# Turning the first attention weights on TensorE, and an earlier start of the dense layer, in a fused attention and SoLU kernel

## Chip, cores, metric

The kernel runs on one core of a Trainium2 chip. The metric is the device time of one execution in microseconds (us), the median of several runs.

The engines are called by the names of the profile: PE (TensorE, matmul; PEld is its weight load), DVE (VectorE), ACT (ScalarE), POOL (GpSimd), SP (SyncE, which issues most DMAs).

## Reference

```python
# q, k, v: (8, 8, 576, 64) float32; tau a scalar
scores = scale * np.matmul(q, k.transpose(0, 1, 3, 2))
thresh = np.max(scores, axis=-1, keepdims=True) - tau
scores = np.where(scores >= thresh, scores, -1000000000.0)
attn = softmax(scores); x = attn @ v        # heads side by side: (4608, 512)
h = x @ w_in                                # w_in (512, 1024)
solu = h * softmax(h)
ln = (solu - mu) / np.sqrt(var + 1e-06) * g_ln
out = ln @ w_out                            # w_out (1024, 512)
```

`w_in` and `w_out` arrive as 64-bit floats. The kernel reads them as 64-bit integers and makes 32-bit floats of them itself.

## The kernel before

**Work units.** Two heads make a pair (`NP` = 4 pairs a batch, 32 in all). A slot is one step of attention: 128 score rows by 576 columns for each of two heads. A batch has 18 slots: for each of two `kind`s (row blocks) four pairs `hp` with two slots `r` = 0, 1, and two slots of kind 2 for the rows left over. Eight batches make 144 slots. Two slots r = 0, 1 of a pair form a unit, whose weights are then multiplied with v. After the four units of one kind, 256 tokens of x are complete; they are two token tiles of 128 for the dense layer. There are 36 such tiles. (0, 0, 0), (0, 0, 1), (0, 1, 0) and (0, 1, 1) are the first four; the text calls them T0 to T3.

**Rounds.** The loop from line 855 emits one round per slot, r0 to r143, and then some rounds without a slot. The order in the queue of each engine is the order in which this loop emits the instructions. In a round `rnd`:

- PE: `scores` (L434) into two PSUM tiles `s0`, `s1`. Beside them, in the free columns 576 to 1023, `turn_beside` (L379) may turn k and q of a later pair with the identity. Then comes either half of `ff_h` (L605 or L595: x times w_in into `h_ps`) or half of `ff_o` (L710: times w_out into `o_ps`), and, when one is due, the `pv` of a unit (L542).
- DVE: `maxes` (L455, two passes that give the row threshold), the copies of turned k and q in part, `blocks` (L501, two 32x32 block transposes of the slot before), the dense layer's passes (L620 maximum, L635 product, L650 statistics, L676 normalise, L697 transpose), and the weight conversion of one piece (L282, L286, L308).
- ACT: `ramp` (L470, which reads the scores and so frees `s0`, `s1`), `exps` (L479, with row sums), copies of pv (L572), L263 and L340 for the weights, L629 and L671 for the dense layer.
- POOL: `normalise` of the slot before (L486, L487: the inverse of the sums; L489: two passes over w), `weight_c` (L332), small steps of the dense layer.

**Weights to v.** After `blocks` has transposed blocks of 32x32 within the partitions, `wT` is built by three DMAs a unit (L510, L512), which move the blocks between partitions. `pv` follows when `pv_due` says so: `LAG_PV` = 3 rounds after the unit's second slot, and in some cases one more (L751).

**PSUM.** Besides `s0` and `s1` there are two tiles, `p0` and `p1`, handed out by `take` (L104) in the order in which they are given back: for pv, h, o and the early turns.

**Start.** Pair 0 is turned ahead of the loop, pairs 1, 2, 3 by `whole_pair` (L394) in rounds 0, 2 and 4, with both tiles of `take`. Pairs 4 to 7 are turned beside the scores (`preps`, L757) from r14 and r19. Pairs 8 to 31 are turned by DVE and DMA. One of the 16 pieces of weights (128x512) is converted in each of the rounds to r14; L282 and L286 make the mantissa, ACT's L263 the rest of the exponent. `gains` (L216) turns g_ln in round 3.

**Steps of the dense layer.** `ready` holds complete token tiles; `cur` and `prev` with `quarter` walk through h first half, h second half, o first half, o second half. In the loop of before T0's h comes in r11 and r12, T1's in r13 and r14, T0's o in r17 and r18, T2's h in r20 and r21, T1's o in r22 and r23.

Of the kernel before, what the change touches and what calls it, by code (L numbers as in the profile page):

```python
# [20 lines left out]
def kernel(  # L21
# [60 lines left out]
    gs = const.tile([P, NC], F32, name="gs")  # L82
    lims = [const.tile([P, 1], F32, name=f"lim{x}") for x in range(2)]
# [109 lines left out]
    def constants(spread):  # L193
# [4 lines left out]
        make_identity(nc, ident)  # L198
        nc.gpsimd.memset(mhalf, -0.5)
# [16 lines left out]
    def gains():  # L216
        tag, g_ps = take("g_ps")
# [4 lines left out]
        pairs_free.append(tag)  # L222
# [52 lines left out]
    def weight_m(x):  # L275
# [5 lines left out]
        if in_bits(x):  # L281
            nc.vector.tensor_scalar(  # L282
                out=m.bitcast(F32), in0=hi.bitcast(F32), scalar1=2.0**-112, scalar2=None,
                op0=ALU.mult,
            )
            nc.vector.tensor_scalar(  # L286
                out=m, in0=m, scalar1=0x7FFFFFFF, scalar2=3,
# [6 lines left out]
        )  # L294

# [88 lines left out]
    def keep(room, i, nm, ms, by_act):  # L384
        of = room[:, 0 : 64 * len(ms)].rearrange("p (m x a) -> p m a x", a=2, x=32)
        to = pair(i)[nm + "T"].rearrange("p (a m x) -> p m a x", a=2, m=NK)[:, ms[0] : ms[-1] + 1]
        if nm == "k":
            (nc.scalar.copy if by_act else nc.vector.tensor_copy)(out=to, in_=of)
# [22 lines left out]
    def scores(s, items):  # L411
# [4 lines left out]
        x = S  # L416
        for i, nm, ms in items:
            for j in range(2):
                room = ps[j][:, x : x + 64 * len(ms)]
                turn_beside(room, i, nm, ms, j)  # L420
                kept.setdefault(j, []).append((room, i + j, nm, ms))
            x += 64 * len(ms)
        for ks in (slice(SM, S), slice(0, SM)):
            for h in range(2):
                for y in range(2):
# [11 lines left out]
                    )  # L437
        live[s] = dict(ps=ps, kept=kept)
# [44 lines left out]
    def normalise(s):  # L483
# [3 lines left out]
        nc.gpsimd.tensor_tensor(out=sm, in0=sm, in1=mone, op=ALU.pow)  # L487
        for x, w in enumerate(d["w"]):
# [4 lines left out]
    def blocks(s):  # L493
# [6 lines left out]
        for h, w in enumerate(live.pop(s)["w"]):  # L500
            nc.vector.transpose(out=T[:, :, r, h, :], in_=w)  # L501
# [18 lines left out]

    def attend_steps(key):
# [3 lines left out]
        unit["y"] = take("pv")  # L525
# [3 lines left out]
        for e in range(2) if kind == 2 else [None]:  # L529
            for m in range(NK):  # L530
                for u in range(2):
                    d, h0 = source(b * NP + (hp if e is None else e + 2 * u))
                    for h in range(2):
                        if e is None:
# [81 lines left out]

    def ff_max(t):
# [4 lines left out]
    def ff_exp(t):  # L622
# [3 lines left out]
        tag = "xh1" if rnd > NS and len(starts) % 2 else "u"  # L626
# [426 lines left out]
```

## Time and profile before

| | us |
|---|---|
| median of 3 runs | 857.41 |
| the three runs | 859.64, 857.41, 855.07 |
| span of the profiled execution | 854.9 |
| PE busy in it | 819.9 (96%) |
| DVE busy | 674.6 (79%) |
| ACT busy | 570.0 (67%) |
| POOL busy | 496.1 (58%) |

The time of the profiled execution is known only as its span, from its first to its last instruction. "Busy" of PE counts the matmuls with modelled ends, so it is not PE at its peak. The granted clock is the share of full speed that PE was given in a stretch. Every fp32 matmul stands in the trace as two records.

### The profile page before, as it was taken

Reading aid. Unit: us, or ns where it says so; the run is one execution under the profiler, and the core shown is the slowest. Engines: PE = TensorE matmul, PEld = TensorE weight load, DVE = VectorE, ACT = ScalarE, POOL = GpSimd, SP = SyncE. Lnnn points to the kernel's source line nnn. Section 1 sums busy time; section 2 is a strip of 40 time slices with the busy share of each in tenths; the row PEclk is TensorE's granted clock in tenths of the full one; section 3 lists DMA queues with packets and bytes.
Section 4 is the critical chain, followed back from the end, with each engine's and each line's share of the span. In section 5 each row is a group of like instructions: output and inputs, shape, how many; then the busy total and the mean of one; then the engine's idle time right before and its main releaser. Section 6 shows DMA issues by size and latency. Waiting matters only on the chain.

```text
span 854.9 us, 36109 instructions
## 1 busy us (share of the span) xinstructions
PE 819.9 (96%) x15363; PEld 620.5 (73%) x15363; DVE 674.6 (79%) x1225; ACT 570.0 (67%) x1127; POOL 496.1 (58%) x945
## 2 busy tenths in 40 slices
PE   6778899999999999999999999999999999999997
PEld 5555677778677787777688877777777777777655
DVE  5997787989788888888788878888888878787361
ACT  6886876777767666667666666666677777775121
POOL 4885656666566656565566666565666655555120
PEclk8899999999999999999999999999999999999999
DMA  9999778798888888887888778887788887655212
GB/s 343 254 249 213 191 194 233 188 259 204 226 229 202 211 185 218 216 216 190 201 215 218 195 177 209 207 217 207 195 221 226 207 188 175 165 137 140 67 38 63
DMA packets 75314, 168.54 MB, mean 197 GB/s; under 512 B 11146, under 2 KB 32658, under 8 KB 75154
## 3 DMA queue, kind: packets, MB, share of 16 engines
q1 hardware_dynamic: 74866, 165.82, 76.7%
q8 instruction: 120, 1.97, 1.0%
q10 hardware_dynamic: 288, 0.43, 0.2%
q14 instruction: 40, 0.33, 0.1%
HBM read 46.14 MB, written 9.44 MB: 65 GB/s over the span
## 4 chain that ended last, share of the span: by engine, by line
PE 83%; DMA 4%; DVE 4%; ACT 3%; issue 2%; POOL 2%; SPq 1%; DVEq 0%; ACTq 0%; POOLq 0%
PE o_ps L710 27%; PE h_ps L605 22%; PE s_ps L434 15%; PE pv L542 14%; DMA wT<-T 3%; PE h_ps L595 3%; ACT w L470 1%; DVE w L455 1%; ACT w L479 1%; DVE T L501 1%; POOL w L489 1%; POOL sm L487 0%; PE s_ps L379 0%; DVE w L308 0%; PE tp L371 0%
## 5 line engine op out<-in xcount | busy, mean ns | idle before, releaser
L710 PE MATMUL o_ps<-w,uT 64*64 64x256 f32 x4608 | 269.5, 376 | 2.2 <-issue 1.6
L470 ACT ACTIVATE w<-s_ps,nth 128x576 f32<-128x576 f32 x280 | 196.8, 738 | 105.6 <-DVE nth L455 88.6
L455 DVE CUSTOM_DVE_ANT_0 w<-s_ps,tau_t 128x576 f32<-128x576 f32 x280 | 200.0, 751 | 83.5 <-PE s_ps L434 52.4
L710 PEld LDWEIGHTS o_ps<-w,uT 64*64 64x64 f32 x4608 | 221.8, 133 | 55.4 <-ACT xh L572 12.0
L489 POOL TENSOR_SCALAR w<-w,sm 128x576 f32<-128x576 f32 x288 | 220.6, 778 | 14.3
L501 DVE STREAM_TRANSPOSE T<-w 128x576 f32<-128x576 f32 x288 | 207.7, 756 | 22.6 <-POOL w L489 22.3
L605 PE MATMUL h_ps<-w,xh 64*64 64x512 f32 x1856 | 220.8, 589 | 0.0
L479 ACT ACTIVATE w<-w,ntau 128x576 f32<-128x576 f32 x288 | 219.6, 767 | 0.0
L542 PEld LDWEIGHTS pv<-wT,v 64*64 64x64 f32 x5760 | 172.6, 136 | 39.8 <-issue 16.7
L434 PE MATMUL s_ps<-kT,qT 64*64 64x512 f32 (+1 forms) x2048 | 175.8, 416 | 13.4 <-ACT w L470 11.3
L542 PE MATMUL pv<-wT,v 64*64 64x128 f32 (+1 forms) x5760 | 173.9, 263 | 8.3 <-DMA wT<-T 7.4
L605 PEld LDWEIGHTS h_ps<-w,xh 64*64 64x64 f32 x1856 | 118.4, 133 | 77.2 <-issue 43.6
L486 POOL TENSOR_SCALAR sm<-sm 128x2 f32<-128x2 f32 x144 | 34.2, 237 | 186.5 <-ACT w L479 182.8
L487 POOL TENSOR_TENSOR sm<-sm,mone 128x2 f32<-128x2 f32 x144 | 106.7, 741 | 12.0
L434 PEld LDWEIGHTS s_ps<-kT,qT 64*64 64x64 f32 x2048 | 72.7, 137 | 21.7 <-ACT w L470 16.2
L572 ACT COPY xh<-pv 128x256 f32<-128x256 f32 x64 | 25.4, 396 | 80.9 <-PE pv L542 80.9
L671 ACT ACTIVATE V<-u,nb,rs 128x1024 f32<-128x1024 f32 x36 | 44.7, 1240 | 40.5 <-POOL nb L661 33.6
L697 DVE STREAM_TRANSPOSE uT<-V 128x1024 f32<-128x1024 f32 x36 | 44.1, 1225 | 15.9 <-DMA V<-u 15.6
L479 ACT ACTIVATION_READ_ACCUMULATOR w<-w,ntau 128x1 f32 x288 | 55.4, 192 | 0.0
L676 DVE TENSOR_SCALAR u<-u,rs,nb 128x1024 f32<-128x1024 f32 x36 | 34.9, 971 | 19.5 <-ACT V L671 17.9
L635 DVE TENSOR_TENSOR u<-h_ps,u 128x1024 f32<-128x1024 f32 x36 | 42.8, 1190 | 9.4 <-ACT u L629 9.4
L620 DVE TENSOR_REDUCE hm<-h_ps 128x1 f32<-128x1024 f32 x36 | 42.9, 1193 | 4.9 <-PE h_ps L595 2.7
(77 smaller groups left out, 553.5 us busy)
## 6 DMA issues: line engine op xcount, KB each, us to landing
wT<-T SPq DMA_DIRECT2D x160, 288.0 KB, 6.5
wT<-T SPq DMA_DIRECT2D x64, 576.0 KB, 5.5
v<-in_v_dram SPq DMA_DIRECT2D x16, 576.0 KB, 6.0
V<-u SPq DMA_DIRECT2D x144, 64.0 KB, 3.5
out_dram<-ob SPq DMA_DIRECT2D x71, 128.0 KB, 2.6
q<-in_q_dram SPq DMA_DIRECT2D x28, 288.0 KB, 6.1
k<-in_k_dram SPq DMA_DIRECT2D x27, 288.0 KB, 6.4
qT<-flip SPq DMA_DIRECT2D x48, 144.0 KB, 3.2
```

The costliest lines, as they stand in the source:

```text
L434: nc.tensor.matmul(out=ps[h][ROWS[y], ks], lhsT=lhsT, rhs=d["kT"][ROWS[h], ks], start=True, stop=True,)
L455: nc.vector.tensor_tensor_reduce(out=w, in0=ps[:, 0:S], in1=(zero if loose else tau_t).to_broadcast([P, S]), scale=1.0, scalar=BIG, op0=AL ...
L470: nc.scalar.activation(out=d["w"][x], in_=d["w"][x] if d["loose"] else d["ps"][x][:, 0:S], func=AF.Prelu, bias=d["nth"][x], scale=-1.0, al ...
L479: nc.scalar.activation(out=w, in_=w, func=AF.Exp, bias=ntau, scale=1.0, accum_out=sm[:, x : x + 1])
L487: nc.gpsimd.tensor_tensor(out=sm, in0=sm, in1=mone, op=ALU.pow)
L489: nc.gpsimd.tensor_scalar(out=w, in0=w, scalar1=sm[:, x : x + 1], scalar2=1.0, op0=ALU.mult, op1=ALU.mult)
L501: nc.vector.transpose(out=T[:, :, r, h, :], in_=w)
L542: nc.tensor.matmul(out=to, lhsT=d["v"][ROWS[u], (h0 + h - u) % 4, m,], rhs=rhs, start=m == 0, stop=m == NK - 1,)
L605: mm = nc.tensor.matmul(out=h[ROWS[y], f], lhsT=x[ROWS[r], c, ROWS[y]], rhs=w1_parts[ROWS[r], c, part ^ r], start=part == 0 and c == 0, st ...
L671: nc.scalar.activation(out=V, in_=u, func=AF.Identity, bias=nb, scale=rs)
L697: nc.vector.transpose(out=uT, in_=d["V"].rearrange("p y (m x) -> p m y x", x=32))
L710: nc.tensor.matmul(out=d["o"][ROWS[z], 512 * (r ^ other) : 512 * (r ^ other) + 256], lhsT=d["uT"][ROWS[r], m].rearrange("p y x -> p (y x)" ...
```

## The change

1. **The first eight slots** (`FLIPS` = 8; kind 0 of batch 0, four units) no longer pass through L489, `blocks` and the wT DMAs. POOL multiplies a constant `fold` (two 32-column pieces of the identity added up, 128x64) with the inverse sums of each head, which gives a 128x64 matrix with the factors at the places to which the rows go. PE multiplies 64x64 pieces of w with it: 36 matmuls a slot (9 column groups, 2 heads, 2 row halves). This turns, scales and moves the rows in one step. DVE copies the result from PSUM to `wT`: two copies of 64x128 and one of 128x1024. The matmuls of a slot stand in the round after it, behind a pv where one is due; the copies stand at the end of that round.
2. **Slots 8 to 17** keep `blocks`; L538 writes T in another order, since k of these pairs is now held in another column order.
3. **Pairs 2 and 3** are loaded by `load_four` (8 DMAs in place of 4) and turned beside the scores in rounds 1, 2 and 3, behind the scores of that round (`s <= NK`), with ACT's copies between its two ramps. `whole_pair` stays for pair 1 only.
4. **Weights:** for pieces 3 to 8 the pass L282 goes from DVE to POOL (`weight_s`, issued two rounds ahead of its piece, with the result in the final buffer).
5. **g_ln** is loaded behind q of pair 0 and turned before the scores of r0.
6. **The dense layer's first steps** follow a table. T0's and T1's h are cut into four chunks by the contraction (one pair each, two matmuls of 128x128 by 512), in r9 to r13, beside the pv's of rounds 9 and 13. T0's o comes in r16 and r17. r18 has no step. T1's maximum, exponential and product come in r13 and r14, its o in r22 and r23 as before. From r19 on PE's instructions stand in the same order in both kernels.

```diff
+    fold = const.tile([P, 64], F32, name="fold")
...
+        for g in range(2):
+            nc.gpsimd.tensor_tensor(
+                out=fold[:, 32 * g : 32 * g + 32], in0=ident[:, 32 * g : 32 * g + 32],
+                in1=ident[:, 96 - 32 * g : P - 32 * g], op=ALU.add,
+            )
...
+    def weight_s(x):
+        if in_bits(x):
+            hi = raws[x]["raw"].bitcast(F32).rearrange("p (n two) -> p n two", two=2)[:, :, 1]
+            dst = piece(x)[1]
+            nc.gpsimd.tensor_scalar(
+                out=dst, in0=hi, scalar1=2.0**-112, scalar2=1.0, op0=ALU.mult, op1=ALU.mult
+            )
+            raws[x]["scaled"] = dst.bitcast(I32)
...
+        if s > NK:
+            prepare()
         for ks in (slice(SM, S), slice(0, SM)):
...
+        if s <= NK:
+            prepare()
...
+        if s < FLIPS:
+            dg = work.tile([P, NB, 2, 2, 32], F32, tag="T", name="T")
...
+            for x in range(2):
+                nc.gpsimd.tensor_scalar(
+                    out=dg[:, x], in0=fold, scalar1=sm[:, x : x + 1], scalar2=1.0, op0=ALU.mult, op1=ALU.mult
+                )
+            return
...
+    def flip(s, extra):
...
+        tag, room = take("flip")
+        outs = [[room[ROWS[u], P * m : P * m + P] for u in range(2)] for m in range(NK - 1)]
+        outs.append([extra[ROWS[u], 512 * u + 256 : 512 * u + 384] for u in range(2)])
+        for m in (NK - 1, *range(NK - 1)):
+            for h, w in enumerate(d["w"]):
+                for u in range(2):
+                    nc.tensor.matmul(
+                        out=outs[m][u][:, 64 * h : 64 * h + 64], lhsT=w[ROWS[u], 64 * m : 64 * m + 64],
+                        rhs=d["dg"][ROWS[u], h], start=True, stop=True,
+                    )
...
+        def keep_flip():
+            for u in range(2):
+                nc.vector.tensor_copy(out=to[ROWS[u], NK - 1], in_=outs[-1][u])
+            nc.vector.tensor_copy(
+                out=to[:, 0 : NK - 1].rearrange("p m n -> p (m n)"), in_=room
+            )
+            pairs_free.append(tag)
...
+    def ff_chunk(t, c):
+        x = tokens(t)
+        if c == 0:
+            tag, h = take("h_ps")
+            ffn[t] = dict(h=h, tag=tag)
+        for part in range(2):
+            nc.tensor.matmul(
+                out=ffn[t]["h"][:, 512 * part : 512 * part + 512], lhsT=x[:, c],
+                rhs=w1_parts[:, c, part], start=c == 0, stop=c == NP - 1,
+            )
...
+    FLIPS = 8
+    T0, T1, T2, T3 = (0, 0, 0), (0, 0, 1), (0, 1, 0), (0, 1, 1)
+    STEPS = {
+        9: [("c", T0, 0)], 10: [("c", T0, 1), ("c", T0, 2)], 11: [("c", T0, 3), ("c", T1, 0)],
+        12: [("c", T1, 1), ("c", T1, 2)], 13: [("c", T1, 3)],
+        16: [("o", T0, 0)], 17: [("o", T0, 1)],
+    }
+    FREE = max(STEPS) + 1
+    U_HOME = {T1: "xh3"}
...
+    pv_at = [4, 6, 8, 9, 13, 15, 16, 19]
...
-        whole = {0: 1, 2: 2, 4: 3}
+        whole = {0: 1}
...
+            if 0 < rnd <= FLIPS:
+                if due:
+                    due = False
+                    key = pv_due.pop(0)[1]
+                    for _ in attend_steps(key):
+                        pass
+                    evict = flip(rnd - 1, units[key]["y"][1])
+                    attended(key)
+                else:
+                    spare, extra = take("extra")
+                    evict = flip(rnd - 1, extra)
...
+            if rnd + 3 <= FLIPS:
+                weight_s(rnd + 3)
+            if spare is not None:
+                pairs_free.append(spare)
+            if evict is not None:
+                evict()
```

More of the change, by code (lines that the diff above doesn't have):

```diff
@@ L524, in attend_steps @@
         wT = unit["wT"]
-        unit["y"] = take("pv")
+        if "y" not in unit:
+            unit["y"] = take("pv")
         _, y = unit["y"]
@@ L897 @@
                     pairs_free += tags
[L898 removed]
+                idle = not planned if rnd < FREE else quarter == 0 and cur is None and (
                     prev is None or bool(pv_due) and pv_due[0][0] <= rnd
```

124 lines of the change are left out of this document (82 added, 42 removed).

## The prediction

> **What bounds the kernel now.** I read the page first (span and the strip of slices), then the busy time by stretch, cut where DVE starts its first score pass (L455) of a round: one round is one slot of 128 score rows, and r0 to r143 are all the slots. The columns are span, then busy time and instruction count of PE, PEld, DVE, ACT and POOL, the granted clock, the DMA share and GB/s.
>
> ```profile
> span 854.9 us, 36109 instructions
> ```
>
> ```profile
> 117.24:854.90 737.66, 728.29 (x13650) 553.27 (x13642) 581.02 (x1041) 482.11 (x953) 418.67 (x820) 1.00 0.76 190
> 13.67:52.16 38.49, 26.86 (x440) 18.75 (x442) 36.45 (x74) 33.17 (x68) 31.48 (x42) 0.80 0.97 284
> 52.16:89.52 37.36, 31.25 (x548) 22.79 (x545) 29.99 (x59) 26.47 (x54) 26.66 (x42) 0.93 0.93 214
> 89.52:117.24 27.72, 23.81 (x572) 18.40 (x567) 21.45 (x40) 21.53 (x43) 16.96 (x29) 0.94 0.80 190
> ```
>
> The first row is the kernel from r20 to the end: PE 728.29 of 737.66, 99%, at full clock. Nothing that leaves PE's work there alone can make it more than 9.4 us shorter. The other rows are the start. Stage A (r1 to r8, 38.49 us, 4.81 a round) has DVE at 95% and PE at 70% with a clock of 0.80. Stage B (r9 to r14, 37.36 us) and stage C (r15 to r19, 27.72 us) have no full engine. In A the groups of instructions (count, busy, mean ns, then idle time ahead and what ended it) say what PE waits for, and what DVE and POOL do:
>
> ```profile
> L308 DVE SCALAR_TENSOR_TENSOR w<-raw,em 128x512 int32<-128x512 int32 x8 | 7.7, 963 | 0.0
> ...
> L434 PE MATMUL s_ps<-kT,qT 64*64 64x64 f32 x64 | 5.8, 272 | 10.8 <-ACT w L470 10.7
> ...
> L371 PE MATMUL tp<-ident,q 64*64 64x64 f32 x72 | 4.4, 299 | 0.0
> ...
> L371 PE MATMUL tp<-ident,k 64*64 64x64 f32 x72 | 3.7, 264 | 0.0
> ```
>
> ```profile
> L501 DVE STREAM_TRANSPOSE T<-w 128x576 f32<-128x576 f32 x16 | 11.8, 770 | 1.5 <-POOL w L489 1.3
> L489 POOL TENSOR_SCALAR w<-w,sm 128x576 f32<-128x576 f32 x16 | 11.7, 747 | 0.8
> ```
>
> PE's 10.8 us of idle time are the waits for the score banks, which ACT's ramp (L470) frees. In that hole the new matmuls can lie.
>
> **Where a gain can come from.** The built order of both kernels is the same from the scores of r19 on, on PE, and within a round of that on the other engines. The early h steps therefore do not take a step off the end: both kernels enter r20 with the same work left. The change is worth what it moves the start of r20, now at 117.24 us, and no more. I cost A, B and C.
>
> **Prices.** Rows of the whole run by shape, then single rows:
>
> ```profile
> L282 DVE TENSOR_SCALAR em<-raw 128x512 f32<-128x512 f32 x16 | 7.3, 456 | 4.5 <-DMA raw<-in_moe_w_in_dram 4.1
> ...
> L379 PE MATMUL s_ps<-ident,q 64*64 64x64 f32 x144 | 5.1, 232 | 2.5 <-ACT qT L390 2.0 <-ACT w L470 0.5
> L379 PE MATMUL s_ps<-ident,k 64*64 64x64 f32 x144 | 4.7, 220 | 0.3 <-DVE both L455 0.3
> ...
> L388 DVE COPY kT<-s_ps 128x128 f32<-128x128 f32 x1 | 0.3, 285 | 0.0
> ```
>
> ```profile
> 102.19 3.69 PE L710 MATMUL o_ps<-w,uT 64*64 64x256 f32 x64 [0.59 <-ACT xh L572]
> 105.69 1.16 PE L434 MATMUL s_ps<-kT,qT 64*64 64x64 f32 x16
> ```
>
> ```profile
> 784.41 2.13 PE pv L542 x72
> 786.54 3.63 PE h_ps L595 x8
> ```
>
> ```profile
> L671 ACT ACTIVATE V<-u,nb,rs 128x1024 f32<-128x1024 f32 x36 | 44.7, 1240 | 40.5 <-POOL nb L661 33.6
> ...
> L635 DVE TENSOR_TENSOR u<-h_ps,u 128x1024 f32<-128x1024 f32 x36 | 42.8, 1190 | 9.4 <-ACT u L629 9.4
> L620 DVE TENSOR_REDUCE hm<-h_ps 128x1 f32<-128x1024 f32 x36 | 42.9, 1193 | 4.9 <-PE h_ps L595 2.7
> ```
>
> *Flip of a slot:* 36 matmuls of 64x64x64, and each fp32 matmul is two records, so 72 records of the shape of L371 and L379. By L379, (5.1 + 4.7)/288 = 34 ns each, 2.45 us; by L371 in stage A, (4.4 + 3.7)/144 = 56 ns, 4.05 us. The second is the price at a low clock. I take 2.45 and keep 4.05 for the range. *Its copies:* 128x1024 from PSUM is not in the trace; L635 and L620 read as much in 1.19, so 1.2; two of 64x128 at up to 0.285 each. Together 1.75 us less overlaps, where two transposes took 2 x 0.77 = 1.54. DVE is hardly relieved: it gains one weight pass (0.46, rounds 1 to 6, now on POOL) and loses about 0.2. *POOL:* the two 0.75 passes over w go; two of 128x64 (between the 0.22 of a 128x2 pass, below, and 0.75; I take 0.3, the smaller size) and one weight pass of 128x512 (at most 0.75) come. About even. *DMA:* four wT transfers go, of which none ended a wait in A. *Chunk:* half of the 3.63, 1.8 us; a pv of one unit 2.1; a half of o 3.5; scores 1.2; a turn of 56 records 1.9.
>
> **Stage A.** A flip needs the reciprocal sums. In r8:
>
> ```profile
> 47.31 0.75 DVE L455 CUSTOM_DVE_ANT_0 w<-s_ps,tau_t 128x576 f32<-128x576 f32 x1
> ```
>
> ```profile
> 51.19 0.22 POOL L486 TENSOR_SCALAR sm<-sm 128x2 f32<-128x2 f32 x1 [0.42 <-ACT w L479]
> 51.49 0.85 POOL L487 TENSOR_TENSOR sm<-sm,mone 128x2 f32<-128x2 f32 x1
> 52.44 1.47 POOL L489 TENSOR_SCALAR w<-w,sm 128x576 f32<-128x576 f32 x2
> ```
>
> From the first pass to the first use of the sum are 52.44 - 47.31 = 5.1 us; with the two diagonals 5.7. So the flip of slot s can start about 1 us into round s+1. On PE it stands behind the scores, the turn and the pv of that round, and **ahead of the next scores**; behind it on DVE stands its copy, which is ahead of the next first pass. So the flip is now inside the loop that sets the round:
> - rounds with a pv (4, 6, 8): pv 2.1 + flip 2.45 + scores 1.2 = 5.8 on PE;
> - rounds without (5, 7): DVE sets them, 1.5 (two passes) + 0.96 (L308) + 0.46 + about 1.65 = 4.55;
> - r1 to r3, with the turns of pairs 2 and 3 behind the scores and their copies between ACT's two ramps:
>
> ```profile
> 85.40 0.96 ACT L388 COPY kT<-s_ps 128x448 f32<-128x448 f32 x2
> ```
>
> r1, the average of 4.8 with this 0.96 on ACT and part of its turn and its flip added: 6.4, an estimate. r2: 1.2 + 1.7 + 2.45 = 5.4. r3 about the same less the shorter turn: 5.2.
>
> Sum 3 x 5.8 + 2 x 4.55 + 6.4 + 5.4 + 5.2 = 43.5 against 38.5: **5.0 us lost**.
>
> **Stage B.** Here a stall goes:
>
> ```profile
> 72.10 0.44 PE L542 MATMUL pv<-wT,v 64*64 64x128 f32 x4 [2.24 <-DMA wT<-T]
> ```
>
> ```profile
> 78.37 0.76 DVE L455 CUSTOM_DVE_ANT_0 w<-s_ps,tau_t 128x576 f32<-128x576 f32 x1 [4.86 <-PE s_ps L434]
> ```
>
> PE waits for the transfer in a pv, the scores of r13 stand behind that pv, and DVE's first pass of r13 waits 4.9 us for them. In the new order that pv comes a round later and four transfers fewer are ahead of it, so I take the stall as gone. What is late next is DVE: the weight passes run until r14, and T1's maximum and product, which were in C, come into r13 and r14. Statistics:
>
> ```profile
> 85.32 1.28 DVE L650 BATCH_NORM_STATS2 bs<-u 128x6 f32<-128x512 f32 x2
> ```
>
> r9: chunk 1.8 + pv 2.1 + scores 1.2 = 5.1 on PE. r10: two chunks 3.63 + 1.2 and a little = 5.0. From r11, DVE's 4.6 (its round of before) and more: r11 and r12 one 1.19 each, 5.8; r13 1.19 + 1.4, 7.2. r14: ACT carries T1's exponential, T0's V (1.24) and two copies (0.96) ahead of its second ramp, which frees the banks for the turn and scores of r15: about 7.2. Sum 36.1 against 37.4: **1.3 us won**.
>
> **Stage C.** r15 5.4 (ramps, copies, turn, scores in a row). r16: o 3.5 + pv 2.1 + scores 1.2 = 6.8 on PE. r17: 3.5 + 1.2 = 4.7. r18 has no step on PE, so the loop from scores over both ramps to the turn and scores of r19 stands bare: 5.9. r19 as before: 3.7. Sum 26.5 against 27.7: **1.2 us won**.
>
> **Sum:** 5.0 - 1.3 - 1.2 = 2.5 us later, a span of 857.4. The three runs have a median of 857.41, 2.5 above the span, so 859.9, rounded to **860 us**. g_ln's transfer (4 KB) and turn go where PE waits for ACT anyway; cost nothing, and 0.2 us without that cover.
>
> **The clock.** The flips' price hangs on it:
>
> ```profile
> 30.00:33.00 3.00, 2.33 (x62) 1.45 (x56) 2.96 (x6) 3.00 (x8) 2.40 (x5) 1.00 0.82 290
> 36.00:39.00 3.00, 1.19 (x12) 0.31 (x12) 2.93 (x7) 2.67 (x7) 1.64 (x4) 1.00 0.98 239
> 39.00:42.00 3.00, 2.22 (x18) 1.25 (x22) 2.61 (x5) 3.00 (x7) 2.88 (x4) 0.68 0.94 341
> 18.00:21.00 3.00, 3.00 (x48) 2.58 (x42) 2.83 (x8) 1.88 (x5) 2.25 (x4) 0.50 1.03 407
> ```
>
> After a stretch with PE busy for 1.19 of 3 us the clock falls to 0.68; after 2.33 of 3 it holds. With flips PE is busy for over 3.6 of 4.55 us in every round of A, so I take it as full. [...]
>
> **Rivals.**
> 1. *Every stage runs at its busiest engine's sum* (faster). A: 8 x 1.2 scores + 144 x 0.034 turns + 8 x 2.45 flips + 3 x 2.1 pv = 40.4 on PE; B: 33.8 on DVE (r9, r10 and r14 at 4.6, 4.6 and 5.8); C: 24.2 on PE. Sum 98.4 against 103.6, so 852; with flips at 2.2, 850; with the pv's waits gone too, 848. For it: PE runs ahead of DVE in the steady part with no idle time. Against: the copy stands on DVE between flip and next first pass. It decides if PE's idle time in A falls under 2 us.
> 2. *The clock stays at 0.80 in A* (slower). Flips at 4.05: 8 x 1.6 = 12.8, of which the rounds without pv hide some 2: 871. For: the row 18 to 21. Against: the row 30 to 33. It decides once PE's busy share in a round falls to about half.
> 3. *POOL is late.* The new weight pass stands ahead of the next sums on POOL and needs its weights landed. Three rounds of 1 to 2 us late are 3 to 5 more, and nothing hides them since the flip is in the loop: 864.
>
> **How the numbers follow.** The forecast has 0.44 (854 to 866), rival 1 0.26, rival 2 0.14, rival 3 0.16. About 0.5%, 4.3 us, is what a measurement can tell from no change: 853.1 to 861.7. Faster: 0.23 of rival 1 and 0.02 of the forecast, 0.25. Slower: 0.10 of the forecast, 0.14, and 0.11 of rival 3, 0.35. Same: 0.40. The range, 848 to 870, takes in the best of rival 1 and nearly all of rival 2.
>
> **What would show it.** Right: r9's first pass starts at 56 to 58 us, not 52.2; PE busy over 90% from 20 to 57 us at a clock of 1.0; flips in about 2.4 us; no wait for wT near r13; r20 at 118 to 121; 738 us from there to the end. Wrong: r9 before 52 (rival 1); a clock under 0.9 in A with flips over 3 us (rival 2); PE's flips waiting for POOL's T (rival 3); or a part from r20 on that differs by more than 2 us from 737.66, which would say that the same order does not take the same time.

## The result, and the profile after

The changed kernel takes 868.38 us (median of four runs, 866.56 to 873.0), the kernel before 857.55 beside it (855.07 to 859.64). The ratio is 1.0123, with an interval of 1.008 to 1.0165: **slower by 1.2%**. The profiled executions have spans of 865.5 and 854.9 us.

The busy time by stretch of the changed kernel, cut at the first score pass (L481) of r1, r2, r9, r15 and r20, with the columns of the rows of before:

```profile
19.34:30.17 10.83, 6.97 (x144) 6.03 (x147) 4.50 (x11) 4.31 (x9) 8.02 (x13) 0.68 1.02 328
30.17:66.91 36.74, 32.66 (x877) 26.07 (x871) 33.57 (x66) 27.69 (x59) 21.49 (x37) 1.00 0.42 125
66.91:101.93 35.02, 29.23 (x387) 15.70 (x389) 32.23 (x61) 28.60 (x56) 29.12 (x44) 0.88 0.72 177
101.93:127.58 25.65, 24.12 (x574) 20.70 (x570) 18.09 (x37) 19.34 (x41) 13.03 (x23) 0.89 0.75 194
127.58:865.50 737.92, 728.16 (x13650) 550.43 (x13642) 581.23 (x1040) 482.69 (x951) 420.13 (x820) 1.00 0.77 190
```

From r20 on nothing has changed (737.92 against 737.66). B and C together are 60.67 us where they were 65.08. The loss stands in the first row and ahead of it: r1 begins at 19.34 us, not 13.67, and lasts 10.83 us. In it PE is busy for 6.97 us and DVE for 4.50, while the DMA share is 1.02. The starts of the rounds (us, from the rows of the first pass in DVE's timeline; the last column is the rest of the span from r20) in all profiled executions of this study:

| kernel | r0 | r1 | r2 | r3 | r9 | r15 | r20 | r20 to end |
|---|---|---|---|---|---|---|---|---|
| before | 9.5 | 13.7 | 19.3 | 24.2 | 52.2 | 89.5 | 117.2 | 737.7 |
| **changed** | 10.7 | 19.3 | 30.2 | 35.4 | 66.9 | 101.9 | 127.6 | 737.9 |
| e1 one DMA for two pairs | 10.7 | 25.5 | 42.9 | 51.0 | 82.2 | 117.3 | 141.6 | 738.7 |
| e2 g_ln late | 10.4 | 19.3 | 28.0 | 33.7 | 65.9 | 100.7 | 125.6 | 740.6 |
| e3 no weight pass on POOL | 11.0 | 19.4 | 26.4 | 34.1 | 65.5 | 100.5 | 124.8 | 740.3 |
| e4 no flips | 10.2 | 18.4 | 25.8 | 32.3 | 60.9 | 99.0 | 124.7 | 741.3 |
| e5 pairs 2, 3 as before | 10.3 | 16.3 | 22.0 | 30.2 | 66.3 | 101.3 | 126.9 | 741.0 |
| e7 the same, no flips | 10.6 | 16.8 | 21.8 | 26.9 | 55.9 | 92.4 | 118.2 | 737.2 |
| e8 before, loads in halves | 9.5 | 19.9 | 24.3 | 29.2 | 57.2 | 92.3 | 120.0 | 740.9 |
| e9 h in the old rounds | 10.5 | 19.3 | 29.4 | 36.1 | 67.2 | 100.2 | 124.7 | 744.6 |
| e10 before, early steps alone | 10.1 | 15.0 | 19.9 | 24.3 | 52.5 | 89.1 | 114.9 | 740.6 |
| e11 before, g_ln first | 10.9 | 15.8 | 20.7 | 25.1 | 53.2 | 87.6 | 115.7 | 738.6 |
| e12 e10 with POOL's pass | 10.4 | 15.3 | 21.6 | 26.6 | 55.8 | 93.7 | 119.6 | 735.8 |

Each row is one execution. e10 starts as the kernel before does and still has r1 1.3 us later, so differences of about a microsecond in r0 and r1 mean nothing.

**Why r1 is late.** DVE's timeline of the changed kernel (start, duration, instruction, idle time ahead and what ended it):

```profile
14.05 0.43 DVE L290 TENSOR_SCALAR em<-raw 128x512 f32<-128x512 f32 x1 [1.97 <-DMA raw<-in_moe_w_in_dram]
...
18.53 0.43 DVE L290 TENSOR_SCALAR em<-raw 128x512 f32<-128x512 f32 x1 [2.86 <-DMA raw<-in_moe_w_in_dram]
18.99 0.43 DVE L294 TENSOR_SCALAR em<-em 128x512 int32<-128x512 int32 x1
19.34 0.75 DVE L481 CUSTOM_DVE_ANT_0 w<-s_ps,tau_t 128x576 f32<-128x576 f32 x1
```

and of before:

```profile
12.68 0.43 DVE L282 TENSOR_SCALAR em<-raw 128x512 f32<-128x512 f32 x1 [0.16 <-DMA raw<-in_moe_w_in_dram]
13.14 0.43 DVE L286 TENSOR_SCALAR em<-em 128x512 int32<-128x512 int32 x1
13.67 0.76 DVE L455 CUSTOM_DVE_ANT_0 w<-s_ps,tau_t 128x576 f32<-128x576 f32 x1
```

The passes over weight pieces stand ahead of r1's score pass in DVE's queue in both. The last of them waits for its piece of weights to land, at 12.7 us before and at 18.5 after. So the question is why the same weights land 6 us later. The same stretches by 3 us, before and then after:

```profile
9.00:12.00 3.00, 3.00 (x97) 2.70 (x93) 2.39 (x7) 1.88 (x4) 1.07 (x1) 1.00 1.04 415
12.00:15.00 3.00, 1.48 (x23) 0.46 (x18) 2.70 (x6) 3.00 (x7) 0.83 (x2) 1.00 1.05 397
15.00:18.00 3.00, 1.45 (x14) 0.85 (x17) 2.10 (x5) 3.00 (x7) 2.83 (x4) 0.69 1.04 400
```

```profile
9.00:12.00 3.00, 2.27 (x28) 1.15 (x20) 2.89 (x7) 0.69 (x1) 1.19 (x1) 1.00 1.08 235
12.00:15.00 3.00, 2.89 (x56) 2.80 (x54) 0.97 (x5) 2.18 (x4) 0.09 (x1) 1.00 1.02 256
15.00:18.00 3.00, 2.98 (x85) 2.45 (x82) 0.67 (x1) 2.95 (x7) 0.00 (x0) 1.00 1.00 237
18.00:21.00 3.00, 0.63 (x15) 0.49 (x14) 2.44 (x7) 1.54 (x3) 0.58 (x1) 1.00 0.97 252
```

The last two columns are the ones to read. The DMA engines are full in both (share about 1.0), yet they move 245 GB/s on average where they moved 405. Twelve microseconds at 245 instead of 405 leave 12 x (1 - 245/405) = 4.7 us of transfer undone. The trace's packets show it for the whole-partition transfers too: from 9 to 18 us a packet of the weights (4096 bytes) took 164 ns in the median before and 253 ns after.

**Why r1 is long.** POOL's timeline, and PE's, in r1 of the changed kernel:

```profile
20.42 0.65 POOL L308 TENSOR_SCALAR w<-raw 128x512 f32<-128x512 f32 x1 [8.34 <-DMA raw<-in_moe_w_in_dram]
21.15 0.55 POOL L512 TENSOR_SCALAR sm<-sm 128x2 f32<-128x2 f32 x1
21.79 0.93 POOL L513 TENSOR_TENSOR sm<-sm,mone 128x2 f32<-128x2 f32 x1
22.82 0.62 POOL L518 TENSOR_SCALAR T<-fold,sm 128x64 f32<-128x64 f32 x2
```

```profile
23.20 0.78 PE L574 MATMUL extra<-T,w 64*64 64x64 f32 x8 [4.56 <-POOL T L518]
23.76 3.51 PE L574 MATMUL flip<-T,w 64*64 64x64 f32 x61
```

```profile
24.00:27.00 3.00, 3.00 (x64) 3.00 (x62) 0.58 (x2) 0.44 (x1) 2.73 (x6) 0.50 1.02 402
```

POOL's new weight pass waits for its own late piece until 20.42, and the sums of slot 0 stand behind it. Their factors are ready at 23.2; PE has waited 4.56 us for them, the clock has fallen to 0.50, and the flip takes 3.51 us. The scores of r2 and the turn beside them stand behind that flip, so r2 begins at 30.17.

### The profile page after: what moved, and what is told of

Same layout as the page of the kernel before. It is cut to its first block, busy times and chain, and to the rows that moved or that the text cites. A ratio compares the mean times of both kernels' runs of the same rounds, so it can differ in the third digit from the quotient of the medians.

```text
span 865.5 us, 37076 instructions
## 1 busy us (share of the span) xinstructions
PE 834.8 (96%) x15843; PEld 629.9 (73%) x15843; DVE 675.3 (78%) x1227; ACT 571.7 (66%) x1131; POOL 494.6 (57%) x951
## 4 chain that ended last, share of the span: by engine, by line
PE 84%; DVE 5%; DMA 3%; ACT 3%; issue 2%; POOL 1%; SPq 1%; DVEq 0%; ACTq 0%; POOLq 0%
PE o_ps L794 27%; PE h_ps L678 22%; PE s_ps L458 15%; PE pv L615 15%; PE h_ps L668 3%; DVE w L481 2%; ACT w L496 1%; DMA wT<-T 1%; DMA raw<-in_moe_w_in_dram 1%; DMA k<-in_k_dram 1%; PE s_ps L396 1%; ACT w L505 1%; PE flip L574 1%; POOL sm L513 0%; DVE T L536 0%
## 5 line engine op out<-in xcount | busy, mean ns | idle before, releaser
L481 DVE CUSTOM_DVE_ANT_0 w<-s_ps,tau_t 128x576 f32<-128x576 f32 x280 | 200.0, 751 | 81.5 <-PE s_ps L458 50.3
L794 PEld LDWEIGHTS o_ps<-w,uT 64*64 64x64 f32 x4608 | 228.1, 133 | 48.7 <-issue 11.0
L523 POOL TENSOR_SCALAR w<-w,sm 128x576 f32<-128x576 f32 x272 | 209.4, 782 | 13.5
L678 PE MATMUL h_ps<-w,xh 64*64 64x512 f32 x1728 | 203.7, 589 | 0.0
L536 DVE STREAM_TRANSPOSE T<-w 128x576 f32<-128x576 f32 x252 | 181.6, 755 | 19.3 <-POOL w L523 19.2
L615 PEld LDWEIGHTS pv<-wT,v 64*64 64x64 f32 x5760 | 168.8, 135 | 36.1 <-issue 25.2
L615 PE MATMUL pv<-wT,v 64*64 64x128 f32 (+1 forms) x5760 | 169.9, 261 | 3.8 <-issue 3.2
L458 PE MATMUL s_ps<-kT,qT 64*64 64x64 f32 (+1 forms) x2048 | 169.0, 414 | 1.5 <-ACT w L496 1.2
L678 PEld LDWEIGHTS h_ps<-w,xh 64*64 64x64 f32 x1728 | 105.4, 133 | 76.5 <-issue 60.3
L512 POOL TENSOR_SCALAR sm<-sm 128x2 f32<-128x2 f32 x144 | 34.1, 237 | 198.6 <-ACT w L505 195.1
L458 PEld LDWEIGHTS s_ps<-kT,qT 64*64 64x64 f32 x2048 | 67.9, 136 | 6.4 <-ACT w L496 3.1
L755 ACT ACTIVATE V<-u,nb,rs 128x1024 f32<-128x1024 f32 x36 | 44.7, 1241 | 37.1 <-POOL nb L745 31.9
L704 DVE TENSOR_REDUCE hm<-h_ps 128x1 f32<-128x1024 f32 x36 | 42.9, 1190 | 5.5 <-PE h_ps L668 2.7
```

The costliest lines, as they stand in the source:

```text
L458: nc.tensor.matmul(out=ps[h][ROWS[y], ks], lhsT=lhsT, rhs=d["kT"][ROWS[h], ks], start=True, stop=True,)
L481: nc.vector.tensor_tensor_reduce(out=w, in0=ps[:, 0:S], in1=(zero if loose else tau_t).to_broadcast([P, S]), scale=1.0, scalar=BIG, op0=AL ...
L523: nc.gpsimd.tensor_scalar(out=w, in0=w, scalar1=sm[:, x : x + 1], scalar2=1.0, op0=ALU.mult, op1=ALU.mult)
L615: nc.tensor.matmul(out=to, lhsT=d["v"][ROWS[u], (h0 + h - u) % 4, m,], rhs=rhs, start=m == 0, stop=m == NK - 1,)
L678: mm = nc.tensor.matmul(out=h[ROWS[y], f], lhsT=x[ROWS[r], c, ROWS[y]], rhs=w1_parts[ROWS[r], c, part ^ r], start=part == 0 and c == 0, st ...
L755: nc.scalar.activation(out=V, in_=u, func=AF.Identity, bias=nb, scale=rs)
```

## The experiments

Ratios are against the kernel before, measured on the same chip, with 95% intervals. Two theories stood at first: **the transfers** (pairs 2 and 3, loaded in halves of the partitions, slow all that is in flight), and **the loop** (flips, copies and POOL's pass make each round longer, as the prediction had it).

**e1: pairs 2 and 3 in one DMA over all partitions for each tile,** with a destination of 128 partitions filled from two runs of 64 rows.

```diff
+            if i == 2:
+                nc.sync.dma_start(out=raw, in_=heads_of[e])
+                continue
             for j in range(2):
```

> The changed kernel with one edit: k and q of pairs 2 and 3 come in four transfers over all 128 partitions instead of eight over 64. Theory A (the eight transfers over 64 partitions move at about 250 instead of 400 GB/s from 9 to 18 us, and the weights queued behind them land late): r1 starts 3 to 4 us earlier than 19.3, r2 at 21 to 24 instead of 30.2, and the kernel is 5 to 8 us faster than the changed one, 861 to 863. Theory B (the flips in the loop cost it all): r1 and the time stay within 1 us. Theory C (POOL's weight pass ahead of the sums costs it): r1 is the same, and the time within 1 us.

Measured: 882.26 us, ratio 1.0324 [1.0276, 1.0372]; r1 at 25.5 and r2 at 42.9. It was to cure the transfers and made them worse. The busy time of that kernel between 18 and 24 us:

```profile
18.00:21.00 3.00, 0.00 (x0) 0.00 (x0) 0.00 (x0) 0.00 (x0) 0.00 (x0) 1.00 0.17 62
21.00:24.00 3.00, 0.59 (x11) 0.59 (x12) 0.00 (x0) 0.00 (x0) 0.00 (x0) 0.63 0.13 51
```

In the first row every compute engine stands still, in the second all but PE with 0.59 us, while the DMA engines are 17% and 13% busy, about two of sixteen (2/16 = 0.125). The edited transfers fill a tile of 128 partitions from two runs of 64 rows; whether the two runs are what holds the share at about two engines' worth, no run shows. So this was no clean test of the cure, but it shows that the form of these loads alone moves r2 by 12.7 us.

**e2: g_ln loaded behind pairs 2 and 3 and turned in r3, as before.**

```diff
-        nc.sync.dma_start(out=g_rows, in_=g_ln.rearrange("(c p) -> c p", p=P))
...
         load_four(2, "q")
+        nc.sync.dma_start(out=g_rows, in_=g_ln.rearrange("(c p) -> c p", p=P))
...
-        gains(tiles[1][:, 1008:1016])
...
+            if rnd == 3:
+                tag, g_ps = take("g_ps")
+                gains(g_ps)
+                pairs_free.append(tag)
```

> The changed kernel with g_ln loaded behind q of pairs 2 and 3 and turned in r3, as in the kernel before in kind. If g_ln in front delays the first weights (first weight pass at 9.04 instead of 7.03 us), r0 starts 1 to 2 us earlier and the time falls by 0 to 2 us. If it doesn't (my prediction cost it at nothing), the first weight pass stays at 9.0 and the time within 1 us.

Measured: 865.33 us, ratio 1.0128 [1.0079, 1.0177], the same as the changed kernel's. The first weight pass is at 8.9 us and r1 stays at 19.3. g_ln is not what makes r1 late here.

**e3: no weight pass on POOL.** The pass goes back to DVE.

```diff
-            if rnd + 3 <= FLIPS:
-                weight_s(rnd + 3)
```

> The changed kernel with the first weight pass of pieces 3 to 8 back on DVE. Theory C (the pass waits on POOL for piece 3 until 20.4 us with the inverse sums of slot 0 behind it): the first flip starts 3 to 4.5 us earlier than 23.2, r2 starts at 25 to 27 instead of 30.2, and the time falls by 3 to 5 us, less 0.45 a round that DVE gets back in rounds 1 to 6. Theory A alone: the sums come earlier, but the transfers still set r2, so the time falls by less than 1.5 us. Theory B: no change or slower by up to 2.7 us.

Measured: 866.19 us, ratio 1.013 [1.0082, 1.0178]. r1 still begins at 19.4, but r2 at 26.4 instead of 30.2. POOL's timeline:

```profile
17.26 0.24 POOL L512 TENSOR_SCALAR sm<-sm 128x2 f32<-128x2 f32 x1 [4.83 <-ACT w L505]
17.59 0.72 POOL L513 TENSOR_TENSOR sm<-sm,mone 128x2 f32<-128x2 f32 x1
```

The sums now start at 17.26 and not at 21.15, and the first flip begins at 19.1. So the pass does cause r1's length. The 3.8 us are not kept: r2 lasts 7.7 us here (5.2 in the changed kernel), and r9 is 1.5 us earlier in place of 3.8; the time is not clear of the changed kernel's. In r2, PE stops within the turn of q of pairs 2 and 3, and DVE's first pass of r3 waits for that turn, which writes the same PSUM tile:

```profile
33.10 1.07 PE L396 MATMUL s_ps<-ident,q 64*64 64x64 f32 x21 [2.04 <-issue]
```

```profile
34.15 0.76 DVE L481 CUSTOM_DVE_ANT_0 w<-s_ps,tau_t 128x576 f32<-128x576 f32 x1 [3.01 <-PE s_ps L396]
```

The profile names no releaser for PE. It is not the landing of q: its four transfers were issued from 12.1 to 15.5 us, and no load of q to 40 us took more than 9.3 us to land. What PE waited for stays open.

**e4: no flips, all else as changed.** Slots 0 to 7 go through L523, L538 and the wT transfers again; POOL's weight pass stays.

```diff
-    FLIPS = 8
+    FLIPS = 0
...
-    pv_at = [4, 6, 8, 9, 13, 15, 16, 19]
+    pv_at = [5, 7, 9, 10, 13, 15, 16, 19]
...
-            if rnd + 3 <= FLIPS:
+            if rnd + 3 <= 8:
                 weight_s(rnd + 3)
```

> The changed kernel without the flips: the first eight slots go through the block transposes, POOL's passes over w and the transfers, with the first four pv one round later as in the kernel before; loads, g_ln, POOL's weight pass and the early h steps stay. Theory B (the flips in the loop cost 5 us of stage A): r2 to r9 take 4.8 a round, 33.6 instead of 36.7, and the time falls by 3 to 8 us. Theory A or C (the loss of 8 us beyond my prediction lies before r2): r1 stays near 19.3, r2 falls to 25 to 27 since no flip waits for POOL there, and the rest of stage A gains about 3.

Measured: 867.05 us, ratio 1.0137 [1.0073, 1.0201]. r1 is at 18.4 without a flip, so what makes r1 late isn't the flips. r9 is 6.0 us earlier, and it is given back by r20 (2.9 left) and by the end of the span (866.0 against 865.5).

**e8: the kernel before, with pairs 2 and 3 loaded in halves.** Nothing else is changed; each of the four transfers of 128 partitions becomes two of 64.

```diff
+        if i >= 2:
+            for j in range(2):
+                nc.sync.dma_start(out=raw[ROWS[j]], in_=rows_of[nm][P * i + 64 * j : P * i + 64 * j + 64])
+            return
```

> The kernel before with one edit: each load of k and q of pairs 2 and 3 is cut into two transfers over 64 partitions. Theory A' (transfers into 64 partitions slow everything that is in flight with them to about 250 GB/s): the throughput from 9 to 18 us falls from about 400 to 250 GB/s, r1 starts 2 to 5 us later than 13.7, r2 2 to 5 us later than 19.3, and the time grows by 2 to 6 us. If the loads of the changed kernel were slow for another reason (their order, g_ln), the throughput and the time stay within 1 us.

Measured: 861.88 us, ratio 1.0061 [1.0033, 1.009]. r1 is at 19.9 (13.7 before), r9 at 57.2 (52.2). Stretches and the largest wait from 8 to 25 us in total, count and longest:

```profile
9.00:12.00 3.00, 2.07 (x71) 1.96 (x69) 1.93 (x5) 1.27 (x2) 1.27 (x1) 1.00 1.05 210
...
18.00:21.00 3.00, 0.00 (x0) 0.00 (x0) 2.88 (x5) 0.99 (x2) 1.70 (x2) 0.50 1.05 230
```

```profile
DVE em L286 <- DMA raw<-in_moe_w_in_dram: 10.2, 3, 4.6
```

The halves alone bring the changed kernel's picture into the kernel before: a full DMA share at 210 to 250 GB/s, the same wait of DVE for weights (10.7 us in the changed kernel, 10.2 here), the same start of r1. This is the cleanest result of the study: **the form of these loads is enough for all of r1's delay** (6.2 us here, 5.7 in the changed kernel) and for 5.0 us at r9. In the time it is 0.6%, half of the changed kernel's loss. A packet of the weights took 294 ns in the median here, 164 ns before.

**e5: the changed kernel with pairs 2 and 3 loaded and turned as before.** **e7: the same without flips.**

```diff
-        load_four(2, "k")
+        load_pair(2, "k", nc.sync)
+        load_pair(2, "q", nc.sync)
...
-        whole = {0: 1}
+        whole = {0: 1, 2: 2, 4: 3}
```

> The changed kernel with pairs 2 and 3 as in the kernel before: four loads over 128 partitions in the old order, turned in r2 and r4 with both spare PSUM tiles. Theory A': 400 GB/s from 9 to 18 us, r1 at 14 to 15.5 instead of 19.3, r2 at 20 to 22 instead of 30.2; the turns then delay the flips of r2 and r4 by 1 to 3 us each, r9 at 60 to 62 instead of 66.9, and the time falls by 4 to 7 us against the changed kernel. Rival (POOL's weight pass or the flips are the cause): r2 stays over 26 and the time within 2 us.

> The same without the flips: pairs 2 and 3 as before, no flips, but g_ln in front, POOL's weight pass and the early h steps. Theory A' with my forecast of the stages (flips lose in stage A, the early steps win in B and C): stage A near the kernel before, r9 at 53 to 55; from r9 to r20 61 to 64 us instead of 65.0 in the kernel before, r20 at 114 to 118, and the time from 3 us faster to 1 us slower than the kernel before. If the flips are what wins from r9 to r20 (their transfers are gone), r9 to r20 takes 65 or more and the time is 1 to 3 us slower than before.

e5: 869.18 us, ratio 1.0147 [1.0108, 1.0187]. Its transfers are at 393 to 413 GB/s again, and r2 begins at 22.0, 8.2 us earlier. Yet r1 is at 16.3 (14 to 15.5 were expected), r9 at 66.3, and the time has not fallen. At r1 the last weight pass starts at 14.28, not 18.53, but then DVE waits for PE's scores. They stand behind the turns of the rest of pair 0 and of pair 1, which waited for DVE's copy of the turned g_ln (`gs`):

```profile
10.40 3.25 PE L388 MATMUL tp<-ident,q 64*64 64x64 f32 x56 [0.71 <-DVE gs L224]
```

```profile
16.26 0.76 DVE L481 CUSTOM_DVE_ANT_0 w<-s_ps,tau_t 128x576 f32<-128x576 f32 x1 [1.08 <-PE s_ps L458]
```

So whole loads give back 3.1 of r1's 5.7 us. Of the rest, 1.1 us is this wait, and e10, which loads as the kernel before does, is 1.3 us late as well. The rest of the time goes in r2 and r4, where `whole_pair` has both tiles of `take` and the flip needs both. The waits of that kernel between 34 and 47 us:

```profile
DVE wT L582 <- ACT xh L645: 5.0, 1, 5.0
...
PE pv L615 <- ACT qT L409: 3.0, 1, 3.0
```

PE waits until ACT has emptied the turned pair from PSUM, then pv and flip follow, ACT's copy of pv, and then DVE; r4 lasts 11.4 us (5.8 in the changed kernel). This is why the change has to turn pairs 2 and 3 beside the scores, and with the layout for that come the loads in halves. The two ways to turn them take about the same time in the end (869.18 and 868.38 us).

e7: 860.1 us, ratio 1.0053 [1.0023, 1.0083]. r9 is at 55.9, 10.4 us ahead of e5, and all that lies between the two is the flips and the rounds of four pv's. Still 3.7 us are missing to the kernel before at r9, where 53 to 55 was expected, with the transfers of before; and the time is 0.5% longer than before, more than expected. The last runs ask for these 3.7 us.

**e9: h and o in the rounds of before** (no chunks), with the first pv of kind 1 in r12 in place of r13, all else as changed.

```diff
-        9: [("c", T0, 0)], 10: [("c", T0, 1), ("c", T0, 2)], 11: [("c", T0, 3), ("c", T1, 0)],
-        12: [("c", T1, 1), ("c", T1, 2)], 13: [("c", T1, 3)],
-        16: [("o", T0, 0)], 17: [("o", T0, 1)],
+        11: [("h", T0, 0)], 12: [("h", T0, 1)], 13: [("h", T1, 0)], 14: [("h", T1, 1)],
+        17: [("o", T0, 0)], 18: [("o", T0, 1)],
...
-    pv_at = [4, 6, 8, 9, 13, 15, 16, 19]
+    pv_at = [4, 6, 8, 9, 12, 15, 16, 19]
```

> The changed kernel with the dense layer's first steps in the rounds of the kernel before: T0's h in r11 and r12, T1's in r13 and r14, T0's o in r17 and r18, the first pv of kind 1 in r12. If the early steps win what stages B and C won against the kernel before (65.0 - 60.7 = 4.3 us from r9 to r20), r9 to r20 takes 63 to 66 us and the time grows by 2 to 5 us against the changed kernel. If the stages won because the first four units' transfers are gone, r9 to r20 stays at 60 to 62 and the time within 1.5 us.

Measured: 869.82 us, ratio 1.018 [1.0115, 1.0245]. Against what was expected, r9 to r20 is shorter without the early steps (57.5 us, 60.7 in the changed kernel), and the part from r20 on is longer (744.6, 737.9). e1, e2, e3 and e5, which have the chunks too, take 59.4 to 60.7 us there, so the early steps cost about 2 to 3 us ahead of r20 where there are flips. The 6.7 us behind it are from one execution each, and other rows of the table differ by 5 us there.

**e10: the kernel before with the early steps alone. e11: the kernel before with g_ln's load behind q of pair 0. e12: e10 with POOL's weight pass.** e10 and e12 are the changed kernel with its other points taken back (e12 keeps point 4). The edit of e12 on e10:

```diff
+            if rnd + 3 <= 8:
+                weight_s(rnd + 3)
```

> The kernel before with point 6 of the change alone (the table of early dense steps, and T of batch 0 in the other column order): no flips, pairs 2 and 3 and g_ln as before, all weight passes on DVE. Theory (the start is lost through the loads and the weight pass on POOL, the early steps are worth what stages B and C showed): r1 at 13.7 us and r9 at 52 to 53 as before; r9 to r20 62 us as in the run without flips (before 65.0), so r20 at 114 to 115; then 738 or a little less; span 852 to 853, ratio 0.995 to 0.998. Rival (whatever is won ahead of r20 is lost behind it, or the clock falls in stage A and with it the gain): r20 at 117, or 740 and more behind it; ratio 0.999 to 1.004.

> The kernel before with only the load of g_ln moved up behind q of pair 0 (its turn stays in round 3). Theory A (the prediction's: this small transfer costs nothing): r0 at 9.5, r1 at 13.7, ratio 0.998 to 1.002. Theory B (its issue and the transfer stand ahead of the first weights and of pair 1, which is why r0 and r1 are late in the run with pairs as before and no flips): r0 at 10.2 to 10.6, r1 at 15 to 16.8, r9 at 53.5 to 55.5, ratio 1.001 to 1.004.

> The early dense steps with the weight pass on POOL for pieces 3 to 8; g_ln as before. It stands between the run with early steps alone and the run with pairs as before and no flips, which differs from it only by g_ln in front. Theory A (POOL's weight pass makes r1 late, since it waits for landed weights ahead of the sums): r1 at 16 to 17, r9 at 55 to 56, ratio 1.001 to 1.006 against the kernel before. Theory B (g_ln in front does): r1 at 13.7 to 14.2, r9 at 51 to 53, ratio 0.994 to 0.998.

e10: 857.35 us against 856.86, ratio 1.0006 [0.9974, 1.0037]. r9 to r20 takes 62.5 us, as expected (65.1 before), and r20 begins at 114.9. But e11 and e8, which keep the old order there, take 62.4 and 62.8, so this is no gain that can be laid to the early steps. The end does not show it either: 740.6 us follow, the rival's number. A gain of 2.3 us is 0.27%, which the interval neither shows nor excludes. No version of this study beats the kernel before.

e11: 857.15 us, ratio 1.0014 [0.9981, 1.0046]. r0 and r1 are 1.3 and 2.1 us later, but only 0.8 each later than in e10, which has g_ln as before. It costs at most about a microsecond at r9. (Only the load is moved here, not the turn.)

e12: 861.12 us, ratio 1.0045 [1.0011, 1.0079]. r9 is at 55.8, 3.3 us behind e10, and as late as in e7: this is the missing part of e7, and g_ln is none of it. Theory A had r1 begin at 16 to 17. It begins at 15.3, but it lasts 6.3 us, 4.9 in e10: POOL's pass waits for landed weights with the sums behind it, which start at 16.48 (14.42 in e10). So theory A has the cause right and the place one round too early. POOL's timeline of e12, in r1 and in r5, and one row of e10:

```profile
15.75 0.65 POOL L300 TENSOR_SCALAR w<-raw 128x512 f32<-128x512 f32 x1 [3.81 <-DMA raw<-in_moe_w_in_dram]
...
36.59 0.27 POOL L504 TENSOR_SCALAR sm<-sm 128x2 f32<-128x2 f32 x1
36.95 0.71 POOL L505 TENSOR_TENSOR sm<-sm,mone 128x2 f32<-128x2 f32 x1
37.76 1.47 POOL L515 TENSOR_SCALAR w<-w,sm 128x576 f32<-128x576 f32 x2
39.20 1.28 POOL L341 TENSOR_TENSOR w<-w,third 128x512 int32<-128x512 int32 x1
40.45 1.08 POOL L300 TENSOR_SCALAR w<-raw 128x512 f32<-128x512 f32 x1
41.62 0.28 POOL L504 TENSOR_SCALAR sm<-sm 128x2 f32<-128x2 f32 x1
```

```profile
37.69 0.38 POOL L504 TENSOR_SCALAR sm<-sm 128x2 f32<-128x2 f32 x1 [0.70 <-ACT w L497]
```

In r2 to r5 of e12 POOL hardly has idle time: one row of the sums to the next is 5.03 us, and that is the round. In e10 POOL waits for ACT in each round (nine times from 9 to 56 us, 7.9 us together; 1.3 us in e12). Where L515 stays, the weight pass makes POOL the bound, and costs 0.4 us a round from r2 to r5. With the 1.4 us in r1 and 0.3 ahead of it this makes the 3.3 us.

**The times together.** Put alone into the kernel before, the halves cost 0.6% (e8). POOL's pass costs 0.4% on top of e10 (861.12 against 857.35 us), the flips, beside `whole_pair`, 1.1% on top of e7 (869.18 against 860.1). That is more than the 1.2% of the changed kernel, and taken out of it one at a time none of them gives back time that can be told: e3, e4 and e5 have ratios of 1.013, 1.0137 and 1.0147. So each cost is shown, but in another kernel, and they do not add up: what one leaves out, another wait takes (the rows of e3 and e5 show two of them).

## Why the prediction was right, and where it was wrong

The forecast was 860.0 us; 868.38 lies within the range, near its upper end. That is luck: the forecast by itself was to end at 866, and the range goes on to 870 to take in rival 2, a low clock in all of stage A, while the clock was 1.00 from r2 to r8. The forecast's own change (2.5 us later) was too small: the span is 10.6 us later. Against the forecast span of 857.4 the 865.5 measured are 8.1 more, made up as follows.

| term | forecast | measured | difference |
|---|---|---|---|
| start of r1 | 13.67 | 19.34 | +5.67 |
| r1 | 6.4 | 10.83 | +4.43 |
| r2 to r8 | 37.1 | 36.74 | -0.4 |
| stage B | 36.1 | 35.02 | -1.1 |
| stage C | 26.5 | 25.65 | -0.85 |
| from r20 | 737.66 | 737.92 | +0.3 |

**The step that failed first is the start of r1, which was taken as unchanged.** The prediction priced each moved instruction of PE, DVE, ACT and POOL and left the eight loads of pairs 2 and 3 without a price; in its list of the change's parts they appear only through their turns. The strip of stretches that it quoted has the DMA share at 1.03 and 407 GB/s in 18 to 21 us: a full resource ahead of the bound, where a change of form needed a price. e8 shows that price: +6.2 us at r1, from the form alone. From 9 to 21 us e8 moved 210 to 250 GB/s in rows of 3 us and the changed kernel 235 to 256, at DMA shares of 0.97 to 1.08; the kernel before moved 397 to 415, at 1.03 to 1.05. The strip of the prediction also has a row with 239 GB/s at a share of 0.98 (36 to 39 us): that one share can stand beside two rates was there to see, and was not weighed.

**The second is the price of r1.** It is rival 3, POOL's pass ahead of the sums and waiting for landed weights, with the place and the reason as they were written. The rival's size was three rounds of 1 to 2 us late; it was one round, and PE stood for 4.56 us, since the weights were later than in any row of before. It also brought in a piece of rival 2: the clock fell to 0.50 in that wait (0.56 from 22 to 23 us, 0.50 from 23) and the flip took 3.51 us where 2.45 were forecast. e3 takes the pass away and r1 lasts 7.0 us, close to the 6.4.

**The loop was right.** The seven rounds r2 to r8 were to take 5.4, 5.2, 5.8, 4.55, 5.8, 4.55 and 5.8 us and took 5.2, 5.1, 5.8, 4.4, 5.8, 4.6 and 5.8. The prices behind it, in the groups of the changed kernel from r2 to r9:

```profile
L574 PE MATMUL flip<-T,w 64*64 64x64 f32 x448 | 15.0, 219 | 0.5 <-issue 0.5
...
L583 DVE COPY wT<-flip 128x1024 f32<-128x1024 f32 x7 | 8.6, 1225 | 0.2
...
L518 POOL TENSOR_SCALAR T<-fold,sm 128x64 f32<-128x64 f32 x12 | 3.7, 320 | 0.6
L308 POOL TENSOR_SCALAR w<-raw 128x512 f32<-128x512 f32 x3 | 2.6, 871 | 0.0
...
L582 DVE COPY wT<-extra 64x128 f32<-64x128 f32 x8 | 2.3, 285 | 0.1
```

448 records in 15.0 us are 33.5 ns each, so 72 take 2.4 us (2.45 forecast). The copies are 1.23 and 2 x 0.285, 1.8 (1.75); the factors 0.32 (0.3). Only POOL's pass was above its upper bound: 0.87 against 0.75. The clock is 1.00 in this stretch, as forecast, with the flips for about half of PE's work, and rival 2 is wrong from r2 on. PE is 89% busy in it (32.66 of 36.74). Over the whole stretch that was to show over 90% at a clock of 1.0, from 20 to 57 us, it is 82% (30.41 of 37.00) at 0.91, for r1's sake. The two other signs that hang on r1 failed with it: r9 at 66.9, not 56 to 58, and r20 at 127.6, not 118 to 121.

**B and C were right in sum, but the early steps are not shown to be the reason.** The wait for wT is gone, as forecast. In the waits of before from r9 to r15, and in those of the changed kernel:

```profile
PE pv L542 <- DMA wT<-T: 6.1, 4, 2.2
```

```profile
PE s_ps L396 <- ACT kT L407: 5.4, 1, 5.4
```

PE's longest wait is now on ACT: its turn for pairs 4 and 5 waits 5.4 us for ACT's copies, until 97.18 us. That is in r14, where the prediction had ACT too (forecast 7.2 us, measured 7.24). For the rest of B it had DVE, which is busy for 32.23 of the 35.02 us.

The starts of the rounds say where the gain from r9 to r20 goes. The six kernels with flips (changed, e1, e2, e3, e5, e9) take 57.5 to 60.7 us there, the seven without 62.3 to 65.1. Among these seven the early steps make no difference that one execution each can tell: 62.3 to 63.8 with them (e4, e7, e10, e12), 62.4 to 65.1 in the old order (before, e8, e11). And e9, with flips and without early steps, is the shortest of all. So the gain goes with the flips, which take the four units' transfers away (three each, so twelve, not the prediction's four) and bring the first four pv's a round forward. Which of the two it is stays open; the wait for wT alone it is not, since that is gone in e4, e7, e10 and e12 too.

**g_ln at nothing held in the time, but its turn was not free.** It was to lie where PE waits for ACT anyway. Its copy stands on DVE behind the first weight passes, and PE's next turns wait for it (the rows under e5). With whole loads r1's first pass waits for PE's scores by 1.1 us (e5) and 1.2 us (e7). In the changed kernel the weights are later still and hide it, so e2 changes nothing. By r9 it is made up: e7 and e12, which differ in g_ln and in the `fold` that e7 makes and does not use, are 0.1 us apart there.

**Rival 1 is wrong:** it was to hold if PE's idle time in A fell under 2 us, and PE is idle for 3.9 us in r1 and 4.1 from r2 to r9.

**The test by 737.66 was too sharp.** The prediction would have read a difference of 2 us from r20 on as the order taking another time. The rows of the table, e9 aside, range from 735.8 to 741.3, and e8 and e11 differ from the kernel before in their loads alone. One execution can't tell 2 us there.

**The row of 18 to 21 us is part of a longer stretch.** Cut by single microseconds, the clock of the kernel before is 0.50 in each from 17 to 23 us, with PE busy for 0.97 to 1.00 of each, and 1.00 in the next. Rival 2 was to decide at a busy share of about half. In the rows of 3 us of the kernel before, the clock is 0.69 after a row with PE busy for 1.48 us (12 to 15) and 0.68 after one with 1.19 (36 to 39), but 1.00 after two with 1.61 and 1.57 (54 to 60). In e5 it is 1.00 after a row with 0.54 (24 to 27), so the share of one such row does not settle it. The rows of before, then of e5:

```profile
54.00:57.00 3.00, 1.61 (x36) 0.69 (x28) 2.93 (x6) 3.00 (x8) 2.75 (x4) 1.00 0.87 188
57.00:60.00 3.00, 1.57 (x44) 1.36 (x48) 2.90 (x7) 2.98 (x6) 2.90 (x5) 1.00 0.91 285
60.00:63.00 3.00, 3.00 (x66) 2.32 (x62) 2.45 (x6) 2.08 (x6) 2.73 (x6) 1.00 1.05 249
```

```profile
24.00:27.00 3.00, 0.54 (x10) 0.44 (x12) 0.95 (x3) 3.00 (x8) 1.81 (x4) 1.00 1.03 270
27.00:30.00 3.00, 3.00 (x88) 2.42 (x88) 1.55 (x3) 0.43 (x1) 2.37 (x4) 1.00 0.74 284
```

So the chain is: the flips take both spare PSUM tiles in every round; therefore pairs 2 and 3 must be turned beside the scores (e5 shows what it costs not to); the layout for that loads them in halves of the partitions; those loads cut what the full DMA engines move by 40% (245 GB/s in place of 405); the weights land 6 us later; DVE's score pass and POOL's sums stand behind passes over these weights; and only then come the flips, which cost what was forecast. A kernel with the flips and with whole-partition loads in the layout for the turns beside the scores, in a form that keeps all DMA engines busy, wasn't tried (e1 kept about two).

## What to carry to other kernels

Where the DMA share is about 1.0 ahead of the first rounds, price every change in the form of a load by GB/s, as you would an instruction, and see who else is in flight: with loads in halves of the partitions 245 GB/s moved here in place of 405, with the form of e1 62 and 51. Before a step is put into the loop, see what stands ahead of it in the queue of the engine that feeds it, and whether that waits for a transfer. A gain of 2 us at an inner point of the trace is no gain until the time shows it; here the rest of the span varied by 5 us from execution to execution. And before a gain is laid to a part of the change, look at the same stretch in the kernels that don't have that part.

## What the hardware showed that was not expected

- Transfers into 64 partitions kept the DMA share at about 1.0 (0.97 to 1.08) and slowed the whole-partition transfers beside them: 235 to 256 GB/s in all, in place of 397 to 415, and 253 ns in the median for a packet of the weights, in place of 164. The share alone did not tell the slow stretch from the fast one; it has to be read with the GB/s.
- With tiles of 128 partitions filled from two runs of 64 rows, 62 and 51 GB/s moved at shares of 0.17 and 0.13 (18 to 24 us), with the compute engines idle but for 0.59 us of PE (e1).
- After the wait of 4.56 us the granted clock was 0.50 from 24 to 27 us, with PE busy in all of it, and flips took 3.51 us there; the first flip of e3, without that wait, took about 2.0 us. Cut by single microseconds, the clock is 0.50 from 23 to 28 us, 0.52 to 29, and 1.00 from there.
